# Two steps of a first layer in one PSUM bank, earlier slopes, decay tables in shared slots, later weights

## The chip, the cores and the metric

The kernel runs on one core of a Trainium2 chip. The metric is the device time of one execution in microseconds (us). The engines are PE (TensorE matmul) with PEld (its weight load), DVE (VectorE), ACT (ScalarE), POOL (GpSimd) and SP (SyncE, which here only issues DMAs). PE writes its results into PSUM, which has eight banks of 2 KiB per partition; SBUF is the working memory.

## The reference

Three parts follow each other. `x_t` is the transposed output of the first part, cut into tokens.

```
# 1. retention, 4 batches x 8 heads x 576 tokens x 64
scores = q @ k.T / sqrt(64);  ret = (scores * gamma_h ** (i - j) * (i >= j)) @ v
# 2. 2304 tokens x 512, 2048 wide
h = x @ w_in;  g = max(h, 0) + alpha * min(h, 0);  x2 = g @ w_out
# 3. 2304 tokens x 512, 1536 wide
out = (sigmoid(x2 @ w_gate) * (x2 @ w_val)) @ w_out2
```

## The kernel before, in words

The 2304 tokens are cut into five blocks of 256, 512, 512, 512 and 512 tokens (`BLOCKS`). Retention runs in 20 runs of up to 128 tokens of one batch: runs 0 and 1 fill block 0, runs 2 to 6 block 1, four or five runs each of the others. For a run n, POOL scales `qk<n>` by a decay table (`dec<n>`, made by ACT from the constants, line 266) and `kv<n>`; PE makes the scores `s<n>`; DVE masks them; PE makes the output `o<n>` and the running state `m<n>`; DVE adds the state to `m_sb`; ACT and DVE split `o<n>` into a high and a low part of `x<block>` (`split`, lines 131 and 132). Every factor is kept as such a pair, and every product is three matmuls (`products`, line 396).

The middle part has 16 steps f. `h<j>_<f>` is the first layer of block j in step f (12 matmuls), evicted from PSUM by the slope formula and split into `g<j>_<f>`; `y<j>` gathers the second layer over all f (for block 0 in the four halves of two banks, `y0a` and `y0b`). While weights are still to be prepared, the eviction is two Relus on ACT (lines 408 and 409), a scalar_tensor_tensor on DVE with the negated slopes `na_sb` (line 410), a copy on ACT (131) and a subtraction on DVE (132). Afterwards it is two DVE operations, the copy and the subtraction.

Weights come as int64 words of two floats. A raw tile `r` is loaded by SP (line 142) and prepared in two ACT operations (153, 155), three DVE operations (159, 160, 163), an ACT copy (170) and a DVE subtraction (172), which give the pair `w`. `weight_step` moves this preparation on by a fraction; `w1_<f>_0` is needed by `h<j>_<f>`, `w1_<f>_1` by `y<j>`.

Block 0 and the first eleven steps of block 1 run side by side, because block 1 reuses each weight as soon as it is there. Then blocks 1 to 4 pass through the 16 steps while the retention runs of the next block are mixed in. In block 4 the weights of the last part begin to be loaded and prepared. The last part runs all blocks in the order 1, 2, 3, 4, 0.

PE's order is the order of the code. ACT, DVE, POOL and SP have orders that a scheduler set when the program was built; each of them takes its instructions strictly in that order. The `h` tiles share two PSUM banks (`ps_h`): a new `h` waits until the tile before it in its bank has been subtracted (line 132). All large SBUF tiles (`qk`, `kv`, `r`, `w`, `g`) share 38 slots of 4 KiB per partition; the 32 weight tiles of the middle part hold 32 of them from the time they are prepared until block 4. Two of the 256-token `g` tiles share a slot (`half_of_slot`). The decay tables have two buffers of their own.

`y<j>` for j > 0 has the four banks of `ps_y`. At the end of a block each bank is drained to a staging tile `yst` (two buffers) by ACT or DVE and stored; the next block's `y` waits for the drain.

Of the kernel before, what the change touches and what calls it, by code (L numbers as in the profile page):

```python
# [9 lines left out]
F32 = mybir.dt.float32  # L10
F32R = mybir.dt.float32r
U32 = mybir.dt.uint32
I32 = mybir.dt.int32
AF = mybir.ActivationFunctionType
ALU = mybir.AluOpType
# [3 lines left out]
P = 128  # L19
B, H, S, D = 4, 8, 576, 64  # L20
NPAIR = H // 2
NT = B * S
DM = 512
KC = DM // P
NF1 = 2048 // P
NF2 = 1536 // P
BLOCKS = (256, 512, 512, 512, 512)
FIRST = tuple(sum(BLOCKS[:j]) for j in range(len(BLOCKS)))
NBLK = len(BLOCKS)
NSLOT = 38  # L30

ORDER = (1, 2, 3, 4, 0)

# [8 lines left out]

BEHIND = 2

WITH = 3


PACE_B, PACE_C, PACE_E, PACE_F = 0.34, 0.5, 0.65, 1
# [42 lines left out]
def retention_two_ffn(ctx: ExitStack, tc: tile.TileContext, att, cst, alpha, w1, w2, out):  # L91
    nc = tc.nc

    const = ctx.enter_context(tc.tile_pool(name="const", bufs=1))

    big = ctx.enter_context(tc.tile_pool(name="big", bufs=NSLOT))
    xp = ctx.enter_context(tc.tile_pool(name="xp", bufs=2))
    small = ctx.enter_context(tc.tile_pool(name="small", bufs=2))
    dp = ctx.enter_context(tc.tile_pool(name="dp", bufs=1, space=DRAM))
    ps_y = ctx.enter_context(tc.tile_pool(name="ps_y", bufs=4, space=PSUM))  # L100
    ps_h = ctx.enter_context(tc.tile_pool(name="ps_h", bufs=2, space=PSUM))
# [4 lines left out]
    ap = att_only.enter_context(tc.tile_pool(name="ap", bufs=1))  # L106
    c_sb = ap.tile([P, N_CST], F32, tag="c", name="c_sb")
    al_sb = const.tile([P, NF1], F32, tag="al", name="al_sb")
    na_sb = const.tile([P, NF1], F32, tag="na", name="na_sb")
# [5 lines left out]

    def slot(shape, dtype, name):
        return big.tile(shape, dtype, tag="big", name=name)

    halfslot = {}

    def half_of_slot(name):

        t, i = halfslot.pop("t", (None, 0))
        if t is None:
            t = slot([P, 2, 2, DM // 2], F32R, name)
            halfslot["t"] = t, 1
        return t[:, i]

    def split(hi, lo, src):

        nc.scalar.activation(hi, src, AF.Copy)  # L131
        nc.vector.tensor_tensor(out=lo, in0=src, in1=hi.bitcast(F32), op=ALU.subtract)  # L132
# [51 lines left out]
    def load_weights(n):  # L184
        for key in to_load[:n]:
            load_weight(key)
        del to_load[:n]

    def advance():

        for g in list(under_way):
            if next(g, StopIteration) is StopIteration:
                under_way.remove(g)

    def begin_weight():
        if to_prepare and to_prepare[0] in raw_w:
            under_way.append(prepare_weight(to_prepare.pop(0)))
            load_weights(1)

    def weight(*key):  # L200
        while key not in wt:
            begin_weight()
            advance()
        return wt[key]
# [3 lines left out]
    def weight_step(n):  # L208

        credit[0] += n  # L210
        if credit[0] >= 1.0:
            credit[0] -= 1.0
            begin_weight()
        advance()
# [9 lines left out]
    def load_chunk(n):  # L224
        if n >= len(CHUNKS) or n in raw_a:
            return
        load_qk(n)
        load_kv(n)
# [27 lines left out]
    x_t = {}  # L256
    def att_q(n):

        _, _, pos, c, _ = CHUNKS[n]
        by = decay  # L260
        if pos:

            by = ap.tile([P, NPAIR, P], F32, tag="dec", name=f"dec{n}", bufs=2)
            for pr in range(NPAIR):
                g = O_GP + STARTS.index(pos) * NPAIR + pr
                nc.scalar.activation(by[:, pr, :c], decay[:, pr, :c], AF.Copy, scale=c_sb[:, g:g + 1])
        for part in (slice(0, 2), slice(2, 4)) if n == 0 else (slice(0, 4),):
            q = raw_a[n][0][:, 0, part, :c]
            nc.gpsimd.tensor_tensor(out=q, in0=q, in1=by[:, part, :c], op=ALU.mult)  # L269
# [66 lines left out]
    def runs_of(j):  # L336
        return [n for n, ch in enumerate(CHUNKS) if ch[0] == j]
# [6 lines left out]
    def att_stages(j):  # L344

        for n in runs_of(j):
            x_of(n)
            s_sb = att_scores(n, ps_a, "ab")
            load_qk(n + 1)
            yield  # L350
            att_values(n, s_sb, ps_a, "ab")
            load_kv(n + 1)
            if n + 1 < len(CHUNKS):
                att_q(n + 1)
                att_v(n + 1)
            yield

    def att_run(runs, pools, pace, fill):

        scored = []  # L360

        def score(i):
            if i < len(runs):
                n = runs[i]
                x_of(n)
                pool = pools[i % len(pools)]
                scored.append((n, att_scores(n, *pool), *pool))
                if i + 1 < len(runs):
                    att_q(n + 1)
                    att_v(n + 1)  # L370

        def weights(i):
            weight_step(pace(i))
            weight_step(pace(i))

        att_q(runs[0])
        att_v(runs[0])
        score(0)
        for i in range(len(runs)):
            weights(i)  # L380
            att_values(*scored[i])
            fill(i)
            weights(i)
            if i == 0:
                score(1)
            score(i + 2)


    g_t = {}
    y_t = {}  # L390

    def products(ps, pairs, first=True, last=True):

        todo = [(l[:, i], r[:, m]) for l, r in pairs for i, m in ((0, 0), (0, 1), (1, 0))]
        for i, (l, r) in enumerate(todo):
            nc.tensor.matmul(ps, l, r, start=first and i == 0, stop=last and i == len(todo) - 1)  # L396

    def cols(t, k):
        return t[:, :, k * P:(k + 1) * P]

    def ffn1_h(j, f):
        w = weight(1, f, 0)
        nb = BLOCKS[j]
        ps = ps_h.tile([P, nb], F32, tag="h", name=f"h{j}_{f}")
        products(ps, [(cols(w, k), x_t[j][:, :, k]) for k in range(KC)])
        t = small.tile([P, nb], F32, tag="t", name=f"t{j}_{f}", bufs=1)
        if to_prepare:
            nc.scalar.activation(t, ps, AF.Relu)
            nc.scalar.activation(ps, ps, AF.Relu, scale=-1.0)
            nc.vector.scalar_tensor_tensor(ps, ps, na_sb[:, f:f + 1], t, ALU.mult, ALU.add)  # L410
        else:
            nc.vector.tensor_scalar(t, ps, 0.0, al_sb[:, f:f + 1], ALU.min, ALU.mult)  # L412
            nc.vector.scalar_tensor_tensor(ps, ps, 0.0, t, ALU.max, ALU.add)  # L413
        name = f"g{j}_{f}"
        g_t[j, f] = slot([P, 2, nb], F32R, name) if nb > DM // 2 else half_of_slot(name)
        split(g_t[j, f][:, 0], g_t[j, f][:, 1], ps)

    def drain(e, name, ps, dst):
# [29 lines left out]
    def load_x2(j, k):  # L448
        if k == 0:
            x2_t[j] = new_x(j, "x2_")  # L450
        st = small.tile([P, BLOCKS[j]], F32, tag="st", name=f"x2r{j}_{k}")
        nc.sync.dma_start(out=st, in_=x2d[j][:, k, :])
        split(x2_t[j][:, 0, k], x2_t[j][:, 1, k], st)
# [24 lines left out]
    nc.gpsimd.memset(m_sb, 0.0)  # L478
    for n in runs_of(0) + runs_of(1):
        load_chunk(n)  # L480
    nc.sync.dma_start(out=al_sb, in_=alpha)
    nc.scalar.activation(na_sb, al_sb, AF.Copy, scale=-1.0)
    load_weights(4)

    pa, py = (ps_a, "ab"), (ps_y, "yy")
# [1 line left out]
    done = [0]  # L487

    def first_h(i):
        while done[0] < EARLY and done[0] * (n0 + n1 - LATE) < EARLY * (i + 1 - LATE):  # L490
            ffn1_h(0, done[0])
            done[0] += 1
# [7 lines left out]


    att_run(runs_of(0) + runs_of(1), [pa, py, py], lambda i: PACE_B if i >= WITH else 0, first_h)
    weight(1, 0, 1)

# [19 lines left out]
    n = runs_of(2)[0]  # L524
# [3 lines left out]
    for j in range(1, NBLK):  # L528
        stages = att_stages(j + 1) if j + 1 < NBLK else iter(())
        first = step1 if j == 1 else 0  # L530
        total = 2 * len(runs_of(j + 1))
        span = SPAN * (NF1 - first) // NF1
        staged = 0
        if j == NBLK - 1:
            att_only.close()
            extra.append(ctx.enter_context(tc.tile_pool(name="extra", bufs=NEXTRA)))
        for f in range(first, NF1):
            ffn1_h(j, f)
            if j == NBLK - 1:
                if f == 0:  # L540
                    to_load += [(2, f2, m) for f2 in range(NF2) for m in range(3)]
                    to_prepare += to_load
                    load_weights(3)
                if 8 <= f < 8 + KC:
                    load_x2(ORDER[0], f - 8)
                weight_step(PACE_E)
            for point in range(2):
                if staged < total and staged * span < total * (2 * (f - first) + point):
                    next(stages)
                    staged += 1  # L550
                if point == 0:
                    later(BEHIND - 1)
                    if j == NBLK - 1:
                        weight_step(PACE_E)
            late.append((j, f))
        for _ in stages:
            pass
# [58 lines left out]
```

## Time and profile before

| | |
|---|---|
| time, median of 3 runs | 947.21 us (946.84 to 948.4) |
| the profiled execution's own time | 946.92 us |
| its span, first to last instruction | 945.1 us |
| PE busy | 915.4 us (97%) |
| DVE busy, ACT busy, POOL busy | 429.8, 310.8, 45.1 us |
| DMA | 69.86 MB, mean 74 GB/s |
| the chain that ended last, by engine | PE 87%, DVE 6%, ACT 3%, DMA 1%, the rest under 1.5% each |

Time outside the span is 1.8 us. Matmuls are pipelined, so PE's busy share counts the time in which at least one is under way, also where the matmuls run slowly. What can be won or lost lies where PE waits.

### The profile page before, as it was taken

The numbers are of one execution on the slowest core, as the hardware profiler recorded it, in microseconds if no ns is written. First come the engines' busy times: TensorE is split into PE (matmuls) and PEld (weight loads), VectorE is DVE, ScalarE is ACT, GpSimd is POOL, SyncE is SP. The second block draws the span as 40 slices with busy tenths as digits, with TensorE's granted clock in tenths as the row PEclk, the third lists the DMA queues.
The fourth block names the chain that finished last, engine by engine and source line by source line (L and its number), as shares of the span: only waits on it lengthen the run. The fifth ranks groups of instructions, "written<-read, shape, count | busy, mean of one in ns | idle before, by whom it ended". The sixth has DMA issues, their size and how long they took to land.

```text
span 945.1 us, 12323 instructions
## 1 busy us (share of the span) xinstructions
PE 915.4 (97%) x5032; PEld 769.2 (81%) x5032; DVE 429.8 (45%) x726; ACT 310.8 (33%) x604; POOL 45.1 (5%) x46
## 2 busy tenths in 40 slices
PE   6689999999999999999999999999999999999998
PEld 5578888888888888878888888888888888888897
DVE  2989974454443544378787831321122112211212
ACT  3588942221111111157776631211122111211211
POOL 6000001111000000000000000000000000000000
PEclk9799999999999999999999999999999999999999
DMA  9932302332010210145443500200020001000100
GB/s 323 362 100 83 109 23 90 131 103 69 23 57 24 90 45 23 45 160 181 150 155 123 167 1 0 89 1 1 1 74 16 1 1 48 19 1 1 45 1 23
DMA packets 27976, 69.86 MB, mean 74 GB/s; under 512 B 6928, under 2 KB 8464, under 8 KB 27920
## 3 DMA queue, kind: packets, MB, share of 16 engines
q1 hardware_dynamic: 27920, 69.08, 21.6%
q8 instruction: 39, 0.64, 0.3%
q14 instruction: 17, 0.14, 0.0%
HBM read 59.64 MB, written 9.44 MB: 73 GB/s over the span
## 4 chain that ended last, share of the span: by engine, by line
PE 87%; DVE 6%; ACT 3%; DMA 1%; issue 1%; SPq 1%; DVEq 0%; ACTq 0%
PE z L396 31%; PE h L396 18%; PE y L396 17%; PE o L396 16%; PE s L287 1%; DVE r L160 1%; DVE r L163 1%; PE o L326 1%; PE o L306 1%; DVE w L172 1%; ACT r L153 1%; ACT r L155 1%; SPq L253 1%; DMA al_sb<-alpha 1%; DVE h L410 1%
## 5 line engine op out<-in xcount | busy, mean ns | idle before, releaser
L396 PE MATMUL z<-x,w 128*128 128x512 f32 (+1 forms) x1440 | 305.4, 368 | 0.0
L396 PEld LDWEIGHTS z<-x,w 128*128 128x128 f32 x1440 | 252.4, 188 | 45.8
L396 PE MATMUL h<-x,w 128*128 128x512 f32 (+1 forms) x960 | 213.7, 372 | 6.9 <-DVE g L132 5.4
L396 PEld LDWEIGHTS h<-x,w 128*128 128x128 f32 x960 | 167.3, 190 | 39.4 <-DVE g L132 6.4
L396 PE MATMUL y<-g,w 128*128 128x512 f32 x768 | 186.8, 392 | 1.9 <-ACT yst L423 1.9
L396 PEld LDWEIGHTS y<-g,w 128*128 128x128 f32 x768 | 143.2, 188 | 33.4 <-ACT yst L423 2.3
L396 PE MATMUL o<-w,p 128*128 128x512 f32 x648 | 156.8, 389 | 0.0
L463 DVE TENSOR_TENSOR z<-sg,z 128x512 f32<-128x512 f32 (+1 forms) x60 | 38.5, 642 | 258.3 <-PE z L396 258.3
L396 PEld LDWEIGHTS o<-w,p 128*128 128x128 f32 x648 | 120.9, 188 | 24.5
L131 ACT ACTIVATE g<-h 128x512 fp32r<-128x512 f32 (+1 forms) x80 | 44.3, 554 | 199.1 <-DVE h L413 183.0
L462 ACT ACTIVATE sg<-z 128x512 f32<-128x512 f32 (+1 forms) x60 | 33.2, 553 | 169.1 <-PE z L396 168.9
L131 ACT ACTIVATE p<-z 128x512 fp32r<-128x512 f32 (+1 forms) x60 | 33.3, 555 | 132.5 <-DVE z L463 132.5
L412 DVE TENSOR_SCALAR t<-h,al_sb 128x512 f32<-128x512 f32 (+1 forms) x43 | 31.5, 733 | 99.1 <-PE h L396 99.1
L132 DVE TENSOR_TENSOR g<-h,g 128x512 fp32r<-128x512 f32 (+1 forms) x80 | 50.8, 635 | 24.7 <-ACT g L131 22.2
L132 DVE TENSOR_TENSOR p<-z,p 128x512 fp32r<-128x512 f32 (+1 forms) x60 | 38.3, 638 | 33.2 <-ACT p L131 33.1
L160 DVE CUSTOM_DVE_ANT_0 r<-r,t 128x1024 uint16<-128x1024 uint16 x68 | 46.6, 689 | 4.7 <-ACT g L131 0.5
L163 DVE SCALAR_TENSOR_TENSOR r<-r 128x512 uint32<-128x512 uint32 x68 | 46.7, 686 | 0.5
L172 DVE TENSOR_TENSOR w<-r,w 128x512 fp32r<-128x512 f32 x68 | 45.2, 685 | 3.3 <-ACT w L170 3.2
L153 ACT ACTIVATE r<-r 128x512 f32<-128x512 f32 x68 | 45.7, 672 | 1.1 <-DMA r<-w 1.1
L155 ACT ACTIVATE r<-r 128x512 int32<-128x512 uint32 x68 | 45.8, 674 | 0.0
L170 ACT ACTIVATE w<-r 128x512 fp32r<-128x512 f32 x68 | 43.5, 668 | 3.3 <-PE o L396 2.6
L287 PE MATMUL s<-qk 64*128 64x128 f32 (+1 forms) x320 | 24.2, 293 | 10.8 <-POOL qk L269 6.4
(46 smaller groups left out, 506.2 us busy)
## 6 DMA issues: line engine op xcount, KB each, us to landing
r<-w SPq DMA_DIRECT2D x68, 512.0 KB, 3.7
kv<-att SPq DMA_DIRECT2D x16, 512.0 KB, 3.6
qk<-att SPq DMA_DIRECT2D x15, 512.0 KB, 3.9
y<-ost SPq DMA_DIRECT2D x18, 256.0 KB, 2.0
x2d<-yst SPq DMA_DIRECT2D x16, 256.0 KB, 2.3
x2r<-x2d SPq DMA_DIRECT2D x16, 256.0 KB, 2.9
qk<-att SPq DMA_DIRECT2D x6, 256.0 KB, 4.1
kv<-att SPq DMA_DIRECT2D x4, 256.0 KB, 6.2
```

The source lines that it names most:

```text
L131: nc.scalar.activation(hi, src, AF.Copy)
L132: nc.vector.tensor_tensor(out=lo, in0=src, in1=hi.bitcast(F32), op=ALU.subtract)
L153: nc.scalar.activation(high.bitcast(F32), high.bitcast(F32), AF.Copy, scale=2.0 ** -112)
L155: nc.scalar.activation(low.bitcast(I32), low, AF.Copy, scale=2.0 ** -29)
L160: nc.vector.tensor_tensor(out=low.bitcast(I32), in0=low.bitcast(I32), in1=top.bitcast(I32), op=ALU.add)
L163: nc.vector.scalar_tensor_tensor(low, high, 0x80000000, low, ALU.bitwise_and, ALU.bitwise_or)
L170: nc.scalar.activation(w[:, 0, :], low.bitcast(F32), AF.Copy)
L172: nc.vector.tensor_tensor(out=w[:, 1, :], in0=low.bitcast(F32), in1=w[:, 0, :].bitcast(F32), op=ALU.subtract)
L287: nc.tensor.matmul(ps[e][:c, pr, :c], qk[r, 1, pr, :c], qk[r, 0, pr, :c], start=True, stop=True)
L396: nc.tensor.matmul(ps, l, r, start=first and i == 0, stop=last and i == len(todo) - 1)
L462: nc.scalar.activation(t, ps[0], AF.Sigmoid)
L463: nc.vector.tensor_tensor(out=ps[1], in0=t, in1=ps[1], op=ALU.mult)
```

## The change

Five edits:

1. The slopes (`alpha`) are loaded right after the tiles of run 0 instead of after all of the first seven runs, and `na_sb` is computed after run 0's values.
2. The decay tables `dec<n>` take slots of the shared pool, which has 39 instead of 38.
3. During the first seven runs, weights are prepared from run index 4 on instead of 3 (`WITH`).
4. In block 0 two steps of the first layer, f even and f odd, write the two halves of one PSUM bank. The eviction is made once for both, after the odd step, on 512 columns (the scalar_tensor_tensor, whose slope differs, once for each half), and always in the form with ACT. The two `g` tiles are one slot.
5. In block 4 no `weight_step` is made in the first two steps (`LATER`).

```diff
-NSLOT = 38
+NSLOT = 39
...
-WITH = 3
+WITH = 4
+
+LATER = 2
...
-            by = ap.tile([P, NPAIR, P], F32, tag="dec", name=f"dec{n}", bufs=2)
+            by = slot([P, NPAIR, P], F32, f"dec{n}")
...
+    pair = {}
+
+    def ffn1_h0(f):
+
+        w = weight(1, f, 0)
+        nb = BLOCKS[0]
+        if f % 2 == 0:
+            pair["ps"] = ps_h.tile([P, 2, nb], F32, tag="h", name=f"h0_{f}")
+        ps = pair["ps"]
+        products(ps[:, f % 2], [(cols(w, k), x_t[0][:, :, k]) for k in range(KC)], f % 2 == 0, f % 2 == 1)
+        if f % 2 == 0:
+            return
+        t = small.tile([P, 2, nb], F32, tag="t", name=f"t0_{f}", bufs=1)
+        nc.scalar.activation(t, ps, AF.Relu)
+        nc.scalar.activation(ps, ps, AF.Relu, scale=-1.0)
+        for i in range(2):
+            nc.vector.scalar_tensor_tensor(
+                ps[:, i], ps[:, i], na_sb[:, f - 1 + i:f + i], t[:, i], ALU.mult, ALU.add
+            )
+        g = slot([P, 2, 2, nb], F32R, f"g0_{f}")
+        split(g[:, 0], g[:, 1], ps)
+        for i in range(2):
+            g_t[0, f - 1 + i] = g[:, :, i]
+
     def ffn1_h(j, f):
+        if j == 0:
+            return ffn1_h0(f)
...
-        g_t[j, f] = slot([P, 2, nb], F32R, name) if nb > DM // 2 else half_of_slot(name)
+        g_t[j, f] = slot([P, 2, nb], F32R, name)
...
-    nc.sync.dma_start(out=al_sb, in_=alpha)
-    nc.scalar.activation(na_sb, al_sb, AF.Copy, scale=-1.0)
+        if n == 0:
+            nc.sync.dma_start(out=al_sb, in_=alpha)
...
     def first_h(i):
+        if i == 0:
+            nc.scalar.activation(na_sb, al_sb, AF.Copy, scale=-1.0)
...
-                weight_step(PACE_E)
+                if f >= LATER:
+                    weight_step(PACE_E)
...
-                    if j == NBLK - 1:
+                    if j == NBLK - 1 and f >= LATER:
                         weight_step(PACE_E)
```

PE's instructions stand in the same order as before; what a matmul waits for changes. Three places show what moves.

**Place 1**, ACT at the end of the first seven runs (`o6` is the last run's output, `t0`, `h0`, `g0` the eviction of block 0, `t1`, `h1`, `g1` of block 1). Before:

```order
L131 ACTIVATE x1_199<-o5_411 128x4x128
L408 ACTIVATE t0_0_446<-h0_0_433 128x256
L409 ACTIVATE h0_0_433<-h0_0_433 128x256
L131 ACTIVATE g0_0_450<-h0_0_433 128x256
L170 ACTIVATE w1_0_1_453<-r1_0_1_129 128x512
L170 ACTIVATE w1_2_0_464<-r1_2_0_131 128x512
L131 ACTIVATE x1_199<-o6_466 128x4x64
L408 ACTIVATE t0_1_505<-h0_1_492 128x256
```

and in the change:

```order
L123 ACTIVATE x1_199<-o5_396 128x4x128
L123 ACTIVATE x1_199<-o6_446 128x4x64
L406 ACTIVATE t0_1_484<-h0_0_418 128x512
L407 ACTIVATE h0_0_418<-h0_0_418 128x512
L123 ACTIVATE g0_1_489<-h0_0_418 128x512
L162 ACTIVATE w1_0_1_492<-r1_0_1_128 128x512
...
L426 ACTIVATE t1_1_536<-h1_1_523 128x512
L427 ACTIVATE h1_1_523<-h1_1_523 128x512
L123 ACTIVATE g1_1_540<-h1_1_523 128x512
L162 ACTIVATE w1_2_0_545<-r1_2_0_130 128x512
```

The split of `o6` moved ahead of block 0's first eviction, and the copy of weight `w1_2_0` moved from ahead of both of block 1's first evictions to behind them. DVE's order follows.

**Place 2**, PE in the middle of block 0 (`h0_8` and `h0_9` are its steps 8 and 9, `h1_7` is block 1's step 7). Before:

```order
L396 MATMUL h0_9_1157<-x0_136,w1_9_0_996 128x256 x12
L396 MATMUL y0a_567<-g0_8_1083,w1_8_1_1027 128x256 x6
L396 MATMUL y0b_568<-g0_8_1083,w1_8_1_1027 128x256 x6
L396 MATMUL h0_10_1210<-x0_136,w1_10_0_1062 128x256 x12
L396 MATMUL h1_7_1241<-x1_199,w1_7_0_857 128x512 x12
```

and in the change:

```order
L388 MATMUL h0_8_1031<-x0_135,w1_9_0_992 128x256 x12
L388 MATMUL y0a_549<-g0_9_1132,w1_8_1_1027 128x256 x6
L388 MATMUL y0b_550<-g0_9_1132,w1_8_1_1027 128x256 x6
L388 MATMUL h0_10_1169<-x0_135,w1_10_0_1051 128x256 x12
L388 MATMUL h1_7_1193<-x1_199,w1_7_0_883 128x512 x12
```

`y0a` after step 9 read `g0_8` before, from the eviction of step 8, and now reads a tile that is evicted only after step 9, the row just ahead of it. On DVE the operations of that eviction (lines 409 and 124) stand so, with three of weight `r1_13_0` between them:

```order
L409 SCALAR_TENSOR_TENSOR h0_8_1031<-h0_8_1031,na_sb_85,t0_9_1127 128x256
L151 TENSOR_SCALAR t1_13_0_1244<-r1_13_0_1104 128x512
L409 SCALAR_TENSOR_TENSOR h0_8_1031<-h0_8_1031,na_sb_85,t0_9_1127 128x256
L152 ISA r1_13_0_1104<-r1_13_0_1104,t1_13_0_1244 128x512x2
L155 SCALAR_TENSOR_TENSOR r1_13_0_1104<-r1_13_0_1104 128x512
L124 TENSOR_TENSOR g0_9_1132<-h0_8_1031,g0_9_1132 128x512
```

The first product of steps 10 and 11 stands in the same way behind its pair's last step; for the other pairs a step of block 1 (`h1`, `y1`) stands between.

**Place 3**, ACT at the change from block 3 to block 4 (`yst3_0` and `yst3_2` drain two of block 3's four banks, `r2` and `w2` are weights of the last part). Before:

```order
L423 ACTIVATE yst3_0_3490<-y3_0_2852 128x512
L153 ACTIVATE r2_0_2_3426<-r2_0_2_3426 128x512
L155 ACTIVATE r2_0_2_3426<-r2_0_2_3426 128x512
L131 ACTIVATE g4_1_3469<-h4_1_3452 128x512
L170 ACTIVATE w2_0_0_3472<-r2_0_0_3422 128x512
L153 ACTIVATE r2_1_0_3428<-r2_1_0_3428 128x512
L155 ACTIVATE r2_1_0_3428<-r2_1_0_3428 128x512
L153 ACTIVATE r2_1_1_3444<-r2_1_1_3444 128x512
L155 ACTIVATE r2_1_1_3444<-r2_1_1_3444 128x512
L408 ACTIVATE t4_2_3522<-h4_2_3509 128x512
L409 ACTIVATE h4_2_3509<-h4_2_3509 128x512
L423 ACTIVATE yst3_2_3496<-y3_2_2854 128x512
```

and in the change:

```order
L441 ACTIVATE yst3_0_3427<-y3_0_2807 128x512
L145 ACTIVATE r2_0_2_3381<-r2_0_2_3381 128x512
L147 ACTIVATE r2_0_2_3381<-r2_0_2_3381 128x512
L123 ACTIVATE g4_1_3412<-h4_1_3395 128x512
L441 ACTIVATE yst3_2_3433<-y3_2_2809 128x512
```

Seven operations of weights and of the next step no longer stand between the two drains.

## Rows read from the trace of the kernel before

**Rows 1.** 60 to 130 us: PE, PEld, DVE, ACT, POOL busy (count), clock, DMA share, GB/s

```profile
60.00:130.00 70.00, 65.58 (x398) 58.45 (x398) 66.89 (x128) 58.83 (x121) 0.00 (x0) 1.00 0.28 91
```

**Rows 2.** Waits of PE, 50 to 140 us: total, times, longest

```profile
PE h L396 <- DVE g L132: 5.4, 5, 1.9
```

**Rows 3.** PE in order of time; start, duration, [idle before <- releaser]

```profile
50.33 5.49 PE L396 MATMUL h<-x,w 128*128 128x512 f32 x23 [0.97 <-DVE x L132]
...
59.70 3.02 PE L396 MATMUL h<-x,w 128*128 128x512 f32 x12 [1.01 <-DVE g L132]
...
91.89 3.01 PE L396 MATMUL h<-x,w 128*128 128x512 f32 x12 [0.72 <-DVE g L132]
...
113.72 3.02 PE L396 MATMUL h<-x,w 128*128 128x512 f32 x12 [1.93 <-DVE g L132]
...
126.81 3.02 PE L396 MATMUL h<-x,w 128*128 128x512 f32 x12 [1.61 <-DVE g L132]
```

**Rows 4.** All engines in order of time, 108 to 114 us

```profile
108.74 0.88 PE L396 MATMUL y0a<-g,w 128*128 128x256 f32 x6
...
109.38 0.37 ACT L408 ACTIVATE t<-h 128x256 f32<-128x256 f32 x1
111.58 0.48 DVE L410 SCALAR_TENSOR_TENSOR h<-h,na_sb,t 128x256 f32<-128x256 f32 x1
...
113.24 0.42 DVE L132 TENSOR_TENSOR g<-h,g 128x256 fp32r<-128x256 f32 x1
```

**Rows 5.** Groups by shape: count | busy us, mean ns of one | idle before

```profile
L163 DVE SCALAR_TENSOR_TENSOR r<-r 128x512 uint32<-128x512 uint32 x68 | 46.7, 686 | 0.5
L132 DVE TENSOR_TENSOR g<-h,g 128x512 fp32r<-128x512 f32 x64 | 44.1, 689 | 23.3 <-ACT g L131 20.8 <-POOL qk L269 1.4 <-issue 0.4
L131 ACT ACTIVATE g<-h 128x512 fp32r<-128x512 f32 x64 | 38.2, 597 | 184.8 <-DVE h L413 173.3 <-DVE h L410 11.2 <-PE y L396 0.4
L408 ACT ACTIVATE t<-h 128x512 f32<-128x512 f32 x24 | 14.3, 595 | 20.2 <-PE h L396 20.1
L132 DVE TENSOR_TENSOR g<-h,g 128x256 fp32r<-128x256 f32 x16 | 6.7, 419 | 1.4 <-ACT g L131 1.4
L410 DVE SCALAR_TENSOR_TENSOR h<-h,na_sb,t 128x256 f32<-128x256 f32 x13 | 6.3, 486 | 1.3 <-ACT h L409 1.3
```

**Rows 6.** Waits of ACT, 12 to 30 us: total, times, longest

```profile
ACT na_sb L482 <- DMA al_sb<-alpha: 4.2, 1, 4.2
```

**Rows 7.** ACT and DVE in order of time, the first weight and the last split

```profile
18.13 0.87 DVE L320 TENSOR_TENSOR m_sb<-m_sb,m 64x256 f32<-64x256 f32 x2
...
24.57 0.64 ACT L153 ACTIVATE r<-r 128x512 f32<-128x512 f32 x1
...
25.24 0.43 DVE L159 TENSOR_SCALAR t<-r 128x512 uint32<-128x512 uint32 x1 [6.24 <-ACT r L153]
...
49.86 0.42 DVE L132 TENSOR_TENSOR x<-o,x 128x256 fp32r<-128x256 f32 x1
```

**Rows 8.** Stretch of 2 us, columns as in rows 1

```profile
28.00:30.00 2.00, 0.11 (x1) 0.00 (x0) 2.00 (x5) 2.00 (x4) 0.00 (x0) 0.50 1.02 420
```

**Rows 9.** PE in order of time, at the change from block 3 to 4

```profile
419.17 2.07 PE L396 MATMUL y<-g,w 128*128 128x512 f32 x6 [1.89 <-ACT yst L423]
421.04 4.12 PE L396 MATMUL h<-x,w 128*128 128x512 f32 x12
425.01 2.89 PE L396 MATMUL y<-g,w 128*128 128x512 f32 x12
427.74 2.88 PE L396 MATMUL h<-x,w 128*128 128x512 f32 x12
```

**Rows 10.** Stretch of 2 us behind that wait, and the late drain

```profile
421.00:423.00 2.00, 2.00 (x6) 1.57 (x5) 2.00 (x4) 1.19 (x2) 0.00 (x0) 0.50 0.52 117
...
418.49 0.63 ACT L423 ACTIVATE yst<-y 128x512 f32<-128x512 f32 x1
```

**Rows 11.** PE in order of time, the longest wait of the first stage

```profile
27.28 0.82 PE L287 MATMUL s<-qk 64*64 64x64 f32 x14 [4.40 <-DVE x L132]
```

More of the change, by code (lines that the diff above doesn't have):

```diff
@@ L117, in slot @@
         return big.tile(shape, dtype, tag="big", name=name)
[L119 to L127, printed above, removed]
     def split(hi, lo, src):
```

## The prediction

> **What bounds the kernel now.** I began with the page: PE is busy 915.4 of 945.1 us and holds 87% of the chain that ended last, so the question is where PE waits, and what would make it wait elsewhere. PE's waits in order of time put nearly all of its 30 us of idleness ahead of 128 us; behind that it has one wait. Three places matter.
>
> First, the start. DVE stands 6.24 us for the first weight and then works almost without a gap; PE's first product of block 1 (`h1_0`) starts at 50.33, when DVE has subtracted the last split of `x1` (49.86 + 0.42) [rows 3, 7]. That chain hangs on the landing of the first weight `r1_0_0`: ACT takes it up at 24.57, 1.3 us after it had stood 4.2 us for the slopes [rows 6, 7].
>
> Second, blocks 0 and 1 side by side, 60 to 130 us. DVE is busy 66.89 of 70 us, PE 65.58 and ACT 58.83 [rows 1], so three engines are near full, yet PE's idleness in `h` is all for evictions: five waits, 5.4 us in all, for a subtraction of `g`, which frees the PSUM bank that the next `h` needs [rows 2]. They are 1.01 at `h1_2`, 0.72 at `h1_5`, 1.93 at `h1_7` and 1.61 at `h1_8` [rows 3]; the fifth, by subtraction, is 0.15 (`h1_4`). PE never waits there for a weight.
>
> Third, the change from block 3 to 4: PE waits 1.89 us for a drain that ACT makes late (418.49 + 0.63) [rows 9, 10]. The reader is to see what follows: the granted clock is 0.50 in the next 2 us, that is the 1.2 GHz level [rows 10]. From the starts, six `y` matmuls took 1.87 and twelve `h` 3.97 us, where the twelve `y` behind them took 2.73 (427.74 − 425.01) [rows 9]. At that rate the eighteen take 4.10, so the slow stretch costs 1.74 and the wait with it 3.63 us.
>
> **The pairing (edit 4).** What it takes away: with two steps in one bank, `h1` no longer follows an `h0` that is still being evicted. By the order, `h1_5`, `h1_7` and `h1_8` each get a bank whose reader was done earlier: −0.72, −1.93, −1.61.
>
> What it adds: the `g` of an even step comes only with its odd step. For six of the later pairs a step of block 1 stands between the odd `h0` and the first `y0` of the pair: twelve `h` and twelve `y` matmuls of 512 columns, about 5.5 us by [rows 9], against an eviction of 4.4 (below). I allow 0.4 us each at pairs 4/5 and 6/7, where ACT's and DVE's queues are fullest, less 0.15 for `h1_4`; with the −0.72 that makes −0.1 (bounds −0.9, all covered, and +1). Without that cover each would cost what pairs 8/9 and 10/11 cost, where nothing stands between: `y0a` follows `h0_9` and `h0_11` at once (place 2).
>
> There PE waits for the whole eviction on 512 columns. The bare chain is Relu 0.60 and again 0.60 (both as line 408), two scalar_tensor_tensors of 0.49, copy 0.60, subtraction 0.69: 3.5 us [rows 5]. But DVE's order puts three operations of weight 13 between them (0.43, 0.69, 0.69, the middle one, which has no row, taken like line 163) and the first of these waits for ACT; the copy on ACT lies beside two of them [rows 5, 7]. In DVE's order that is 0.60 + 0.60 + 0.49 + 0.43 + 0.49 + 0.69 + 0.69 + 0.69 = 4.7, less about 0.3 since starts follow each other closer than durations tell: 4.4 us. The nearest whole row says the same. Before, the eviction of `h0_9` on only 256 columns took from 108.74 (the next matmul's start on PE) to 113.66 (DVE's subtraction), 4.9 us, with weights between [rows 4]. PE then could run on into `y0` and `h0_10` and stood only 1.93. I take 4.4, bounds 3.3 (bare, with the overlap) and 4.9. Pair 10/11 is priced like 8/9. So +8.8, less about 0.1 each for the queue that PE has anyway, less the 1.93 + 1.61 removed: +5.1 (bounds +2.9 and +6.3).
>
> Behind a wait the clock can fall. Of the waits here 4.40 and 1.89 were followed by 0.50 [rows 8 to 11], 1.93 and 1.61 by none (1.00 in the whole stretch) [rows 1, 3]. By size the new waits are nearest to 4.40; but that one stood where PE was otherwise mostly idle, and in full work one of three fell. So I count one fall of two at the 1.74 of block 4: +1.7 (bounds 0 and +3.5).
>
> What the grouping saves: DVE's subtractions, eight of 0.69 instead of sixteen of 0.42, 1.2 us; ACT's Relus and copies likewise [rows 5]. I cost it at nothing, since PE's waits name evictions in a row, not DVE's total; if DVE's total is the limit after all, it is a rival (below).
>
> The Trainium skill, "Perfetto Trace Analysis", section "Optimizing Scalar/DVE Operations", speaks against the pairing: where Scalar or Vector aren't saturated but cause bubbles on other engines, breaking up instructions may let work complete sooner. The same section says that grouping improves throughput if the engine is saturated. By the first the sum here would be the one that I give, by the second the rival of 943 us; DVE's 66.89 of 70 us with PE's waits on single evictions stands between them, and nearer to the first.
>
> **The start (edits 1 to 3).** The slopes' wait of ACT (4.2) goes, as they are asked for behind run 0's tiles. ACT then has nothing better to do: `r1_0_0` lands behind the same loads as before, so DVE's work still begins near 25. I cost that at nothing (cover: the loads; without it up to −4.2). In DVE's order up to the last split of `x1`, block 0's first eviction (0.49 + 0.42) and two weight subtractions (about 0.65 each) move behind it, and one addition of `m_sb`, 0.87, moves behind the first weight's wait: −2.2 + 0.9 = −1.3, taken as −1.2 [rows 5, 7]. Given back: `h1_1` now follows a bank of a pair not evicted until then, about +0.7 (the bank's subtraction on 512 columns), and `w1_2_0`, moved behind both first evictions of block 1 (place 1), comes later for `h0_2`, whose neighbour waited 1.01 before: I reckon 2.4, two more subtractions of 0.69 on DVE, +1.4 [rows 3, 5]. Sum +0.9 (bounds −0.5, if `w1_2_0` is covered by `y0`, and +2). The decay tables in slots: 39 slots for the same tiles and one or two tables; ACT no longer waits for POOL there (off the path), and blocks 1 to 4 have PE full. Nothing, bounds ±0.3.
>
> **LATER (edit 5).** The drain `yst3_2` comes seven ACT operations sooner (place 3), five of them between 0.60 and 0.67 ahead of it. That is over 3 us against a wait of 1.89, so the wait and the slow clock behind it go: −3.6 (bounds −3.6 and 0, if PE stands at another drain, or the clock falls for another reason). The weights of the last part start two steps later; by the order 24 of them are loaded before the last part and two a step are prepared where three are used, so none is late.
>
> **Sum.** +0.9 − 0.1 + 5.1 + 1.7 − 3.6 = +4.0. Against the profiled execution (946.92, of which the span is 945.1) that is 950.9; the median of the runs is 0.3 above that execution: **951.2 us**.
>
> **Rivals.**
> - *Covered after all:* both new waits are near the bare chain (+2.9 instead of +5.1) and the clock doesn't fall: +0.9 − 0.1 + 2.9 − 3.6 = +0.1, 947.3 with the 0.3 to the median. For it: DVE gets 1.2 us of room. Against: the order puts weight operations inside the chain.
> - *DVE is the limit (the other side):* between 60 and 130 us PE only waits because DVE is full; then a PE wait at `y0` is paid back, as PE finds all later evictions and weights ready, and what counts is DVE's work, −1.2. With +0.9 at the start and −3.6 at block 4: −3.9, 943.3. It decides if DVE, not an eviction in its queue, is what later waits end on; that is, if DVE's backlog at the new waits is over 3 us. For it: 66.89 of 70. Against: no wait for a weight in [rows 2].
> - *The start is won:* with ACT free 4 us sooner the first weight is begun near 19, and DVE's gap of 6.24 closes: −6 on the +4.0, 945.2. That needs `r1_0_0` well before 21 us; against it: DMA stands at 420 GB/s at 28 us still, full [rows 8].
> - *Heavier:* both clock falls (+1.7 more) and block 4's wait stays (+3.6): 956.5. For it: two waits of the size of 4.40; against: the order at place 3.
> - *No effect of LATER alone* (the drain waits for the store instead, which frees its buffer): 954.8, inside the first case's range.
>
> **How the numbers follow.** My forecast 0.50; covered 0.23; heavier 0.12; DVE the limit 0.10; the start won 0.05. What differs from no change by 0.2%, 1.9 us, is all that a measurement of this kernel can tell: 945.3 to 949.1 counts as the same. The forecast and heavier make slower 0.62, covered makes same 0.23, the last two faster 0.15. The range leaves out the case at 943.3, most of that at 945.2 and most of the heavy one, under 0.2 together: 945.4 to 955.5. The forecast's own range, with the bounds of single waits, is 949.1 to 954.8.
>
> **What would show it.** Right: PE waits of about 4.4 us at the first `y0a` after `h0_9` and `h0_11`, ended by DVE's (or ACT's) `g`; no waits at `h1_5`, `h1_7` and `h1_8`; a wait of some 2 us ahead of `h0_2`; `x1`'s last subtraction about 1 us sooner; clock 0.50 after one of the long waits; PE without a wait and at 1.00 between 415 and 428 us. Wrong: PE waits at `y0a` under 3 us, or waits at `y0(4)` and `y0(6)` of over 1 us (then the covered pairs cost too), a wait for a drain at block 4, or DVE starting its first weight well before 24 us.

## The result, and the profile after

The changed kernel takes 958.05 us (median of 4 runs, 957.62 to 958.66) beside 947.81 us for the kernel before (4 runs, one more than in the table ahead): ratio 1.0114, 95% interval 1.0100 to 1.0128. The forecast was slower, 951.2; the time lies 2.5 us above the top of its range. The profiled execution has a span of 956.1 us, 11.0 more than before.

PE's order is the same in both kernels, so the start of the same matmul in the two traces tells how far the changed one is behind. Five rows of PE in order of time, before: `y1` of steps 0, 4, 5 and 6, which stand behind `h1_2`, `h1_6`, `h1_7` and `h1_8`, and the last product of the program.

```profile
62.56 2.88 PE L396 MATMUL y<-g,w 128*128 128x512 f32 x12
103.15 2.88 PE L396 MATMUL y<-g,w 128*128 128x512 f32 x12
116.57 2.88 PE L396 MATMUL y<-g,w 128*128 128x512 f32 x12
129.67 2.88 PE L396 MATMUL y<-g,w 128*128 128x512 f32 x12
...
938.51 2.91 PE L396 MATMUL o<-w,p 128*128 128x512 f32 x12
```

The same five after, with the change of blocks 3 to 4 ahead of the last (its rows answer to [rows 9]):

```profile
65.92 2.88 PE L388 MATMUL y<-g,w 128*128 128x512 f32 x12
107.52 2.88 PE L388 MATMUL y<-g,w 128*128 128x512 f32 x12
125.24 2.88 PE L388 MATMUL y<-g,w 128*128 128x512 f32 x12
142.68 2.88 PE L388 MATMUL y<-g,w 128*128 128x512 f32 x12
...
429.53 3.09 PE L388 MATMUL y<-g,w 128*128 128x512 f32 x12
...
435.19 2.88 PE L388 MATMUL y<-g,w 128*128 128x512 f32 x12
443.99 3.02 PE L388 MATMUL h<-x,w 128*128 128x512 f32 x12 [0.48 <-DVE g L124]
...
949.46 2.91 PE L388 MATMUL o<-w,p 128*128 128x512 f32 x12
```

The differences are +3.36, +4.37, +8.67 and +13.01 us; +13.77 at the `y4` that stood at 415.76 before, +10.18 behind it (425.01 before), +10.95 at the end. So 13 us are lost before 143 us, 3.59 won at block 4, and 1.5 lost elsewhere.

PE's waits of the changed kernel in that first stretch, in order of time (as in [rows 3]):

```profile
53.31 3.02 PE L388 MATMUL h<-x,w 128*128 128x512 f32 x12 [0.91 <-DVE g L124]
59.54 0.50 PE L388 MATMUL h<-x,w 128*128 128x256 f32 x2 [1.78 <-ACT w L162]
...
101.64 0.86 PE L388 MATMUL y0a<-g,w 128*128 128x256 f32 x5 [0.52 <-DVE g L124]
...
116.62 0.58 PE L388 MATMUL y0a<-g,w 128*128 128x256 f32 x1 [3.35 <-ACT g L123]
117.85 1.43 PE L388 MATMUL y0a<-g,w 128*128 128x256 f32 x5 [0.65 <-DVE g L124]
...
134.35 0.38 PE L388 MATMUL y0a<-g,w 128*128 128x256 f32 x1 [3.36 <-ACT g L123]
135.58 1.42 PE L388 MATMUL y0a<-g,w 128*128 128x256 f32 x5 [0.85 <-DVE g L124]
```

The waits of 1.93 and 1.61 [rows 3] are gone, and in their place PE stands 4.00 and 4.21 us for the pair's `g`: first for ACT's copy (the high part), then for DVE's subtraction. Windows of 2 us of the same kernel (columns as in [rows 1]) show what follows the three longest waits:

```profile
60.00:62.00 2.00, 1.72 (x9) 1.68 (x9) 1.86 (x5) 2.00 (x5) 0.00 (x0) 0.64 0.12 20
62.00:64.00 2.00, 2.00 (x8) 1.71 (x7) 1.83 (x4) 2.00 (x4) 0.00 (x0) 0.51 0.65 242
116.00:118.00 2.00, 0.73 (x2) 0.44 (x2) 1.97 (x4) 2.00 (x4) 0.00 (x0) 0.50 0.02 8
118.00:120.00 2.00, 2.00 (x10) 2.00 (x11) 1.94 (x4) 2.00 (x5) 0.00 (x0) 0.50 0.00 0
...
136.00:138.00 2.00, 2.00 (x11) 2.00 (x11) 1.86 (x5) 1.15 (x2) 0.00 (x0) 0.50 0.00 0
```

The granted clock is 0.64 and then 0.51 behind the first and 0.50, the 1.2 GHz level, behind the other two. From 425 to 439 us, around the change of blocks 3 to 4, it is 1.00, and no wait of PE is shown there.

### The profile page after: what moved, and what is told of

Same layout as the page of the kernel before. It is cut to its first block, busy times and chain, and to the rows that moved or that the text cites. A ratio compares the mean times of both kernels' runs of the same rounds, so it can differ in the third digit from the quotient of the medians.

```text
span 956.1 us, 12280 instructions
## 1 busy us (share of the span) xinstructions
PE 920.9 (96%) x5032; PEld 772.9 (81%) x5032; DVE 430.4 (45%) x715; ACT 310.5 (32%) x586; POOL 44.5 (5%) x46
## 4 chain that ended last, share of the span: by engine, by line
PE 87%; DVE 5%; DMA 3%; ACT 2%; SPq 1%; issue 1%; POOL 0%; ACTq 0%; DVEq 0%; POOLq 0%
PE z L388 31%; PE h L388 19%; PE y L388 16%; PE o L388 15%; PE s L279 1%; DMA r<-w 1%; PE o L318 1%; PE o L298 1%; PE y0a L388 1%; DVE r L152 1%; PE y0b L388 1%; DMA x2r<-x2d 1%; DVE r L155 1%; PE m L304 1%; SPq L245 1%
## 5 line engine op out<-in xcount | busy, mean ns | idle before, releaser
L123 ACT ACTIVATE g<-h 128x512 fp32r<-128x512 f32 x72 | 43.0, 597 | 196.6 <-DVE h L431 163.3
L430 DVE TENSOR_SCALAR t<-h,al_sb 128x512 f32<-128x512 f32 x40 | 30.0, 751 | 91.9 <-PE h L388 91.9
L124 DVE TENSOR_TENSOR g<-h,g 128x512 fp32r<-128x512 f32 x72 | 49.6, 689 | 24.3 <-ACT g L123 23.7
```

## The experiments

The theory after the result: four mechanisms make the loss. (a) The pair's eviction stands uncovered in front of `y0(8)` and `y0(10)`. (b) The clock falls behind each long wait, three times. (c) `w1_2_0` comes late for the third step of block 0, from the edits at the start. (d) Decay tables in slots are made late. LATER is a gain. Rivals: the clock has no part, DVE is late anyhow, or the pairing itself carries the late start.

All ratios are to the kernel before, run on the same chip; the 95% interval stands in brackets.

**The pairing alone** (e1_pair_only): the kernel before with edit 4 of the change, its core being:

```diff
+        if j == 0:
+            return ffn1_h0(f)
```

> The kernel before with the pairing alone. By the theory that the pairing itself costs the time (two waits of about 4 us at the first y0a behind steps 9 and 11, each followed by a stretch at the lower clock, 8.6 us net, 1.0 at the other pairs, about 1 us at the bank that the second step of block 1 waits for) it is about 958, and the clock is 0.50 behind both waits. By the rival that edits 1 to 3 at the start carry a third of the loss (w1_2_0 late, clock low behind that wait) it is about 956, with no low clock near 60 us. The wait at the change to block 4 and its 1.74 us behind it should stand here as before, which is in both numbers.

Measured: 958.62 us, 1.0116 [1.0101, 1.0131], all of the changed kernel's loss. Two of its waits of PE:

```profile
114.49 0.38 PE L386 MATMUL y0a<-g,w 128*128 128x256 f32 x1 [3.36 <-ACT g L121]
...
133.09 0.58 PE L386 MATMUL y0a<-g,w 128*128 128x256 f32 x1 [3.36 <-ACT g L121]
```

Both are followed by 0.85 or 0.65 us more for DVE and by windows at 0.50. Around the third step of block 0 no wait for `w1_2_0` stands here, so the pairing doesn't cause that one. The 1.89 us at block 4 stands, with 0.57 to 0.58 as the clock behind it.

**LATER alone** (e2_later_only): the kernel before with, at the two places of block 4:

```diff
+LATER = 2
...
-                weight_step(PACE_E)
+                if f >= LATER:
+                    weight_step(PACE_E)
...
-                    if j == NBLK - 1:
+                    if j == NBLK - 1 and f >= LATER:
                         weight_step(PACE_E)
```

> The kernel before with LATER alone. Theory: the 1.89 us wait for the drain and the slow stretch behind it go, -3.6 us, 944.2. In the changed kernel 0.8 us came back behind it (a wait of 0.48 for an eviction in the third step of block 4); if that is LATER's own, 945.0. Rival, that the wait has another cause than the seven operations ahead of the drain: 947.8, unchanged.

Measured: 945.20 us, 0.9979 [0.9970, 0.9987]: −2.0 us by the ratio, and the rival falls. In its trace the wait at the drain is gone and PE runs on at 1.00. The profiled span is 3.3 us shorter than before, but that execution was the fastest of eleven (943.57); why the runs win only 2.0, less than the 3.63 of wait and clock, stays open.

**All but the pairing** (e3_all_but_pair): the changed kernel with block 0's steps evicted singly.

```diff
-        if j == 0:
-            return ffn1_h0(f)
```

> The changed kernel without the pairing (edits 1, 2, 3 and 5). Theory that the late w1_2_0 and the low clock behind its wait come from edits 1 and 3, since the copy and the subtraction stand late here too: start +2.5, decay tables in slots +0.8, LATER -2.8, together 948.3. Rival, that the late start came from the pair's long eviction: no wait of over 1 us at the third step of block 0, 945 to 945.5.

Measured: 949.99 us, 1.0035 [1.0022, 1.0048], so edits 1 to 3 lose more than LATER wins. The twelve executions scatter from 947.4 to 953.3, and the trace is of the slowest. In it PE waits 1.79 + 0.26 us for `w1_2_0`, and the clock falls behind. It falls behind another wait, too, the one that was 1.93 before:

```profile
62.17 0.51 PE L398 MATMUL h<-x,w 128*128 128x256 f32 x2 [1.79 <-ACT w L172]
...
120.14 4.60 PE L398 MATMUL h<-x,w 128*128 128x512 f32 x12 [2.15 <-DVE g L134]
```

Twelve matmuls that take 3.02 us at full clock [rows 3] take 4.60 behind that wait of 2.15.

The two halves don't add up: the pairing alone costs 0.0116 and all else 0.0035, the whole change only 0.0114. One reason is in the rows: the wait of 2.15 and the 1.58 us of slow clock behind it can't come with the pairing, which takes away that wait. Whether this is all of it stays open.

**Pairs covered** (e4_cover): the changed kernel with the steps of block 1 at other iterations of the loop over f, so that one stands behind each pair.

```diff
+STEPS = (1, 2, 4, 6, 8, 10, 11, 12, 14)
...
-        while step1 < EARLY or (step1 - EARLY) * (NF1 - 1) < (BESIDE - EARLY) * f:
+        while step1 < EARLY or f in STEPS:
```

> The changed kernel with the steps of block 1 placed otherwise beside block 0 (in the iterations 1, 2, 4, 6, 8, 10, 11, 12 and 14), so that one stands behind each pair. Theory, that what costs is that nothing covers the eviction of pairs 8/9 and 10/11: the two waits of 4 us and both slow stretches go, at most 0.6 us of wait stays at each pair, 949.5 to 950.5. Rival, that DVE with its weights is late anyway: waits of 2 us and more stay at these pairs, 954 or more.

Measured: 947.27 us, 1.0001 [0.9992, 1.0010]. This one edit wins back all of the 10.8 us, over 2 us more than expected. By the two traces it is 10.78 us, of which 0.96 lies ahead of `y1(0)`, where PE's order is the same in both. What is left of the two waits, then a wait for a bank at `h1_8` that the changed kernel doesn't have, and the stretch around them (columns as in [rows 1]):

```profile
113.05 0.86 PE L390 MATMUL y0a<-g,w 128*128 128x256 f32 x5 [0.91 <-DVE g L126]
124.71 0.85 PE L390 MATMUL y0a<-g,w 128*128 128x256 f32 x5 [0.18 <-DVE g L126]
...
128.94 3.02 PE L390 MATMUL h<-x,w 128*128 128x512 f32 x12 [1.23 <-DVE g L126]
...
110.00:130.00 20.00, 17.68 (x110) 15.45 (x110) 19.59 (x36) 16.68 (x31) 0.00 (x0) 1.00 0.15 52
```

The clock is 1.00 from 110 to 130 us. DVE, busy 19.59 of these 20 us, didn't put waits of 2 us and more back: that rival falls.

**Work for PE in the two waits** (e5_fill): the changed kernel with matmuls against zero weights, which add nothing to `y1`, ahead of `y0(8)` and `y0(10)`.

```diff
...
+        if f in (8, 10):
+            for _ in range(16):
+                nc.tensor.matmul(y_t[1][0], z_sb, x_t[1][:, 0, 0], start=False, stop=False)
         ffn1_y(0, f)
```

> The changed kernel with 16 more matmuls of 512 columns on PE (about 3.6 us, adding zero to a bank of y1) ahead of the first y0a behind steps 9 and 11, where PE otherwise stands 4.0 and 4.2 us. If the low clock behind the two waits is what PE's standing costs besides the waits, it stays at 1.00 there, and 1.7 to 2 us at each place go though no wait gets shorter: 954 to 954.8. Rival, that the extra is not the clock but work behind the late eviction: 958 as the changed kernel.

Measured: 953.25 us, 1.0058 [1.0044, 1.0072]. The kernel does more and is 5 us faster than the changed one. Its rows in order of time, and two stretches around them:

```profile
106.53 2.88 PE L389 MATMUL y<-g,w 128*128 128x512 f32 x12
...
112.12 3.82 PE L540 MATMUL y<-x,z_sb 128*128 128x512 f32 x16
115.78 0.28 PE L389 MATMUL y0a<-g,w 128*128 128x256 f32 x1
116.88 0.86 PE L389 MATMUL y0a<-g,w 128*128 128x256 f32 x5 [0.82 <-DVE g L125]
...
122.48 2.88 PE L389 MATMUL y<-g,w 128*128 128x512 f32 x12
...
138.44 2.88 PE L389 MATMUL y<-g,w 128*128 128x512 f32 x12
...
112.00:130.00 18.00, 17.18 (x100) 14.96 (x99) 15.40 (x28) 13.56 (x25) 0.00 (x0) 1.00 0.17 60
130.00:140.00 10.00, 9.18 (x52) 7.86 (x51) 6.48 (x12) 5.06 (x9) 0.00 (x0) 1.00 0.01 2
```

From `y1(4)` to `y1(5)` it takes 122.48 − 106.53 = 15.95 us, where the changed kernel took 17.72; from there to `y1(6)` 15.96 instead of 17.44. The eviction is no earlier (116.88 − 106.53 = 10.35 us behind `y1(4)`, in the changed kernel 117.85 − 107.52 = 10.33), and `y0a` still waits for it; the clock is 1.00 throughout. So standing cost 1.77 and 1.48 us more than the time that it lasted. The rest of the 5 us is from other places, shown by the trace alone: the start was 1.0 earlier in this execution, and the wait of 0.48 at block 4 is absent.

**Work for PE in the wait at the third step of block 0** (e9_fill_h02): the changed kernel with

```diff
...
+        if f == 0:
+            for _ in range(14):
+                nc.tensor.matmul(y_t[0][0], z_sb, x_t[0][:, 0, 0], start=False, stop=False)
         if done[0] < NF1:
             ffn1_h(0, done[0])
```

> The changed kernel with 14 more matmuls of 256 columns on PE (about 1.7 us, adding zero to y0) ahead of the third step of block 0, where PE waits 2.06 us for w1_2_0 and the clock is at half behind it. If the low clock near 60 to 64 us follows from that wait, it stays at 1.00 and 1.8 us go: 956.2. Rival: the clock falls there for another reason, or the wait only moves: 958.

Measured: 957.01 us, 1.0100 [1.0083, 1.0117]; the interval overlaps the changed kernel's, so the time alone leaves it open. The trace is clear:

```profile
54.09 3.04 PE L389 MATMUL h<-x,w 128*128 128x512 f32 x12 [0.87 <-DVE g L125]
...
65.16 2.88 PE L389 MATMUL y<-g,w 128*128 128x512 f32 x12
...
62.00:64.00 2.00, 2.00 (x12) 1.73 (x12) 1.83 (x4) 2.00 (x5) 0.00 (x0) 1.00 0.63 233
```

From `h1_1` to `y1(0)` it is 11.07 us, in the changed kernel 65.92 − 53.31 = 12.61; the clock at 60 to 64 us is 1.00. That fall cost 1.54.

**Decay tables in buffers of their own** (e6_own_dec): the changed kernel with

```diff
-NSLOT = 39
+NSLOT = 38
...
-            by = slot([P, NPAIR, P], F32, f"dec{n}")
+            by = ap.tile([P, NPAIR, P], F32, tag="dec", name=f"dec{n}", bufs=2)
```

> The changed kernel with the decay tables in two buffers of their own again, and 38 slots. Theory: a table in a slot is made late, since the slot comes free late, so the two waits of 0.31 us for POOL near 183 and 193 us, worth 0.76, go: 957.3. The order of DVE's first weight changes a little with it, which may move the start by up to 1 us either way. Rival, that the waits have to do with POOL alone: 958, and the two waits stay.

Measured: 956.70 us, 1.0092 [1.0079, 1.0106], on the side expected, but the interval overlaps. The two waits of 0.31 for POOL are gone from the trace. They were worth the step from +13.01 to +13.77 above: from `y1(6)` to that `y4` it is 286.09 us here, as in the kernel before, and 286.85 in the changed one.

**WITH = 4 alone** (e7_with_only), and **the early slopes alone** (e12_alpha_only), each in the kernel before.

```diff
-WITH = 3
+WITH = 4
```

```diff
-    nc.sync.dma_start(out=al_sb, in_=alpha)
-    nc.scalar.activation(na_sb, al_sb, AF.Copy, scale=-1.0)
+        if n == 0:
+            nc.sync.dma_start(out=al_sb, in_=alpha)
...
+        if i == 0:
+            nc.scalar.activation(na_sb, al_sb, AF.Copy, scale=-1.0)
```

> The kernel before with WITH = 4 alone. In all but the pairing (950.0, with LATER worth -2.1 to -2.8 and the tables in slots some +0.8) the start was worth about +4.5. Theory: that is WITH, which moves w1_2_0 behind the first evictions of block 1, so that the third step of block 0 waits some 2 us and the clock falls to half behind it: +3 to +4.5, 950 to 952. Rival, that the early slopes carry it: 947 to 948 here and no wait of over 1 us there.

> The kernel before with the slopes asked for early alone. If the first weight's landing sets the start, nothing changes: 946.7 to 947.8. If the 4.2 us of ACT were worth something, 943 to 946. If it carries the late start of the changed kernel, 950 or more.

Measured: WITH 949.43 us, 1.0024 [1.0015, 1.0033]; slopes 947.20 us, 0.9993 [0.9984, 1.0002]. The wait for `w1_2_0` comes with WITH (1.78 + 0.27 us, 0.50 behind it), less costly than I had put it. The wait of 2.15 with 4.60 behind it, seen in e3_all_but_pair, stands in this trace, too. With the slopes early, ACT waits as long as before, for something else; its waits from 12 to 30 us, which answer to [rows 6]:

```profile
ACT dec L266 <- POOL qk L269: 7.3, 4, 4.1
ACT r L153 <- DMA r<-w: 0.2, 1, 0.2
```

**A version that beats both.** Three kernels from the kernel before, with `STEPS` and LATER as above: with the pairing (e8_pair_cover_later), with the pairing but for the first two steps (e10_pairs_from_2), and without pairing (e11_steps_later). The second has:

```diff
+        if j == 0 and f >= 2:
+            return ffn1_h0(f)
```

> The kernel before with the pairing, the steps of block 1 placed as in e4_cover, and LATER; slopes, tables and weights at the start as before. From e4_cover (947.3) without the late w1_2_0 and its slow stretch (2.5 to 3.3) and without the two waits for POOL (0.8): 943.2 to 944. If the pairing is worth nothing once it is covered, it is not below LATER alone (945.2); if the start of the changed kernel cost nothing, 946.5.

> LATER, the steps placed as in e4_cover, and the pairing from step 2 on, with the first two steps single as before, so that the second step of block 1 doesn't wait for the first pair's eviction (0.9 us in the changed kernel). Theory: 944.0 to 944.5, the fastest; if the first pair costs nothing, equal to the kernel with all pairs (0.9973 of before).

> The kernel before with LATER and with the steps of block 1 placed as in e4_cover, without the pairing. It tells what the pairing is worth once it is covered: if the bank that the pairing leaves free is worth its 1.4 us of waits less, this is 945 to 946, 1 us above the kernel with pairs from step 2 on; if the places of the steps alone do it, the two are equal.

Measured: 945.73 us, 0.9973 [0.9963, 0.9983]; 943.70, 0.9963 [0.9950, 0.9975]; 943.12, 0.9959 [0.9945, 0.9973]. All three beat the kernel before, but none is clear of LATER alone (0.9979 [0.9970, 0.9987]), and the first misses its expected 943.2 to 944. The fastest has no pairing. Two rows of it show its two longest waits behind 100 us, which were 1.93 and 1.61 before; as the steps moved, they stand at `h1_6` and `h1_7`:

```profile
104.54 3.02 PE L400 MATMUL h<-x,w 128*128 128x512 f32 x12 [1.33 <-DVE g L136]
117.02 3.06 PE L400 MATMUL h<-x,w 128*128 128x512 f32 x12 [0.99 <-DVE g L136]
```

In the two kernels with pairs, pair 10/11 still waits, though a step of block 1 stands behind it. e8_pair_cover_later, then e10_pairs_from_2:

```profile
125.08 0.85 PE L390 MATMUL y0a<-g,w 128*128 128x256 f32 x5 [1.66 <-DVE g L126]
...
126.49 1.60 PE L390 MATMUL h<-x,w 128*128 128x256 f32 x12
...
122.76 0.85 PE L400 MATMUL y0a<-g,w 128*128 128x256 f32 x5 [1.65 <-DVE g L136]
...
124.25 5.85 PE L400 MATMUL h<-x,w 128*128 128x256 f32 x24
```

The waits are alike, but only in the second does the clock fall behind it (0.51 from 124 to 126 us): the 24 matmuls at 124.25 take 5.85 us, where the same kind take 4.35 at 1.00 (at 113.70 in that trace). So cover shortens the wait for a pair and does not always remove it.

Against its expectation, pairing from step 2 on is not better than none; the profiled execution lost 1.5 us to that fall, which the kernel without pairs doesn't have. The last two intervals overlap, so whether covered pairing is worth anything at all stays open below 0.2%.

## Why the forecast was right in its sign and too small

The sum forecast +4.0 against the profiled execution, and 10.95 came. By terms:

| term | forecast | measured (rows above) |
|---|---|---|
| start, up to `y1(0)` | +0.9 | +3.36 |
| pairs with a step of block 1 behind | −0.1 | +1.01 |
| pairs 8/9 and 10/11, their clock included | +5.1 + 1.7 | +4.30 + 4.34 |
| decay tables | 0 | +0.76 |
| LATER | −3.6 | −3.59, then +0.77 |

**The main step was right**: PE stands at `y0a` behind `h0_9` and `h0_11` for the whole eviction, 4.00 and 4.21 us where 4.4 were forecast, and the waits at `h1_7` and `h1_8` are gone. e4_cover shows that lack of cover is the cause.

**The step that failed is the clock: "I count one fall of two".** The clock fell behind both waits (1.77 and 1.48 us by e5_fill), and a third time behind the wait for `w1_2_0` (1.54 by e9_fill_h02), which I had priced without a fall although I expected 2.4 us of standing there. Three falls are 4.79 us against 1.74, so 3.05 of the 6.95 that the sum lacks. Without their falls the two uncovered pairs come to 5.39, beside 5.1 forecast. The rows offered for it were right: 4.40 was the nearest, and I set it aside because it stood in the sparse start.

**The start was mis-sized for that reason and no other large one.** The last subtraction of `x1` came at 49.14, 0.72 sooner than in [rows 7] (1.2 forecast); `h1_1` waited 0.91 for the pair's bank (0.7), `h0_2` 2.06 (2.4). Less the 1.01 at `h1_2` that went, these make +1.24, with the fall +2.78 of the 3.36. It is edit 3 that makes `w1_2_0` late (e7_with_only). The first weight was still bound by its DMA, as said: ACT stood 10.91 us for it and began it at 25.21; e12_alpha_only shows ACT's 4.2 us change hands to POOL and nothing won.

**The covered pairs cost 1.1 more than forecast.** The shown waits at `y0a` are what I allowed (0.27 and 0.52 at 4/5 and 6/7), and 0.24 at `y0(3)` for a weight. But each stop costs some 0.25 us beyond the idle time that is shown. Rows of PE of the changed kernel, in order of time, at `y0(4)`, step 6, `y0(5)` and step 7 of block 0:

```profile
88.70 0.28 PE L388 MATMUL y0a<-g,w 128*128 128x256 f32 x1
89.25 0.86 PE L388 MATMUL y0a<-g,w 128*128 128x256 f32 x5 [0.27 <-DVE g L124]
...
90.66 1.60 PE L388 MATMUL h<-x,w 128*128 128x256 f32 x12
92.10 0.88 PE L388 MATMUL y0a<-g,w 128*128 128x256 f32 x6
...
93.54 4.74 PE L388 MATMUL h<-x,w 128*128 128x256 f32 x24
```

`y0(5)` without a wait takes 1.44 us (92.10 to 93.54), `y0(4)` 1.96 (88.70 to 90.66): 0.52 more, of which 0.27 is shown as a wait. The same working gives 0.26 beyond the wait at `y0(3)` and at `y0(6)`.

**Decay tables were costed at nothing**, with the cover "PE is full". The order would have told: with buffers of their own, ACT makes seven tables ahead of the first weight, among them two for the next block's first runs; in slots it makes five, the rest comes late, and PE waits twice. e6_own_dec shows that the slots are the cause.

**LATER gave what was forecast at its place (−3.59)**, and alone it is a gain, though only 2.0 us over the whole. Behind it, the wait of 0.48 at 443.99 appears in the changed kernel and neither in e5_fill, with the same order around it, nor in e2_later_only; in front of the late `g` copy ACT stands 1.6 us for a reload of `x2`. That this DMA decides it is argued, not shown.

The rivals: "DVE is the limit" is refuted by the changed kernel's own rows, where nothing is paid back: it is +8.67 behind the first uncovered pair, +13.01 behind the second and still +13.77 at 429.53. The grouping's 1.2 us of DVE bought nothing that could be measured. "Heavier" (956.5) comes nearest to the time, half by luck: both falls came, but the wait at block 4 that it adds went. "Covered after all" and "the start is won" fall with the waits of 4.00 and 4.21 and the first weight at 25.21. In the sum, 4.9 twice bounds the pairs at +6.1, not +6.3; nothing hangs on it. Of the two rules weighed ahead (the Trainium skill, "Perfetto Trace Analysis", section "Optimizing Scalar/DVE Operations"), the runs agree with the one on breaking up instructions that cause bubbles on other engines: PE's 4.00 and 4.21 us are such bubbles. The Trainium skill states that rule for engines that aren't saturated, though, and here DVE was busy 66.89 of 70 us [rows 1]. That grouping pays on a saturated engine, no run here shows, though DVE was busy 19.59 of 20 us in e4_cover.

## What to carry to other kernels

Work grouped over two steps of a loop becomes available only with the second; look in the order of the waiting engine for what stands between the second step and the first use, at every pair and not on average. Price a long wait of TensorE as its length plus the slow clock behind it (1.5 to 1.8 us a fall here), and put any independent step into it: moving two steps of block 1 by one iteration was worth 10 us. A wait that is taken from an engine off the path only changes hands if the next instruction in its queue can't run yet either.

## What the runs showed of the hardware beyond that

Size alone does not tell whether the clock falls: waits of 1.93 and 1.61 in one trace [rows 1, 3] and of 1.66 in e8_pair_cover_later were not followed by a fall; waits of 1.65 in e10_pairs_from_2, 1.89 [rows 9, 10], 2.06 and 2.15 were. Matmuls that add zero, put into two waits that stay, kept the clock at 1.00 and made the kernel 3.25 us faster by the trace.
